# Folding a small matrix into two weight matrices: 128-row matmuls replaced by 32-row tiles of TensorE

## The chip, the cores and the metric

The kernel runs on one core of one Trainium2 chip. The metric is the device time of one execution in microseconds (us). "PE" is TensorE's matmul stream, "PEld" its weight loads, DVE is VectorE, ACT is ScalarE.

## The reference, cut to what matters

Two branches over the same input are mixed by a gate. The part that the change touches is the feature map of the attention branch:

```python
qkv = (x @ wqkv)...                               # x: 2048 x 512, 32 heads of 16
pq = jnp.einsum('bhsd,hdf->bhsf', q, w_phi)       # w_phi: 32 heads, 16 x 16 each
pk = jnp.einsum('bhsd,hdf->bhsf', k, w_phi)
phi_q = concat([softmax(pq), softmax(-pq)])       # the same for pk
```

The kernel never forms `q` and `k`. It multiplies `w_phi` into the weights first: `wq_p = wq @ blockdiag(w_phi)` and `wk_p` likewise, each 512 x 512. The block-diagonal matrix has blocks of 16 x 16, so a 128 x 128 piece of it is zero outside eight blocks. These two products are "the folds".

The other branch computes `z = gelu(x @ w_in)` in two halves, here called z1 and z2, in 16 row tiles each. The folds are woven between these z tiles.

## The kernel before: the parts that matter

The first stage uses eight banks of PSUM (TensorE's output memory): two singly ("pq", two turns) and six in pairs ("zp", three turns in rotation).

```python
def zp_tile():
    return psA.tile([P, 2, CH], FP32, name="zp", tag=next_turn("zp", 3))

def z1_tile(tt):
    zp = z_mm(tt, w_z1, FH)                 # 8 matmuls of 344 columns into a pair
    nc.scalar.activation(out=z1all..., in_=zp[:, :, 0:HF], func=AF.Gelu_apprx_tanh)

def fold(qk, dt):                           # a quarter of one product
    dst = wq_p if qk == 0 else wk_p
    fps = pq_tile([P, CH])
    for kc in range(NDT):                   # 4 matmuls, 128 rows, 128 columns
        nc.tensor.matmul(fps[:, kc * P:(kc + 1) * P],
            lhsT=wqkT[:, qk * 4 + kc, dt * P:(dt + 1) * P],
            rhs=wphi[:, kc, :], start=True, stop=True)
    if dt % 2 == 1:
        nc.scalar.copy(out=dst[:, dt, :], in_=fps[:, :])
    else:
        nc.vector.tensor_copy(out=dst[:, dt, :], in_=fps[:, :])

for c in range(NCH):                        # four chunks of four row tiles
    ts = list(range(c * 4, c * 4 + 4))
    for tt in ts:
        if c > 0: z2_tile(tt)
        if c >= 2 and tt % 2 == 0: fold(3 - c, (tt % 4) // 2)
    for tt in ts:
        z1_tile(tt)
        if c >= 2 and tt % 2 == 0: fold(3 - c, 2 + (tt % 4) // 2)
    z2_norm(ts)
    ...
# The next stage takes PSUM over in new banks. Its first matmuls are k_tile(0), k_tile(1)
# (wk_p, four of 512 columns each) and v_tile(0).
```

The softmax here doesn't subtract the row's maximum and nothing guards it: scores larger than these inputs give would overflow.

## Time and profile before

| | before |
|---|---|
| time, first three runs | 209.02 us median (208.87 to 209.14) |
| span of the profiled run | 207.5 us |
| 32 fold matmuls, PE time they add | 1.79 us (8 x 224 ns) |
| last z matmul to the first v matmul (start to start) | 1.872 us |

From the page of the kernel before, the line of busy times and the line of the chain of waits by engine:

```profile
PE 203.6 (98%) x1456; PEld 122.5 (59%) x1456; DVE 131.4 (63%) x282; ACT 75.4 (36%) x122; POOL 46.6 (22%) x78
PE 98%; DVE 0%; issue 0%
```

PE is busy for 98% of the span and is also 98% of the chain that ended last. A microsecond taken from any other engine is worth nothing unless PE waits for that engine.

The groups of instructions of the folds in the kernel before (line, engine, operation, output<-input, shapes and count, then busy us and mean ns of one, then idle time ahead and its releaser):

```profile
L319 PE MATMUL pq<-wphi,wqkT 128*128 128x128 bf16 x32 | 3.1, 219 | 0.0
L328 DVE CAST wq_p<-pq 128x512 bf16<-128x512 f32 x2 | 1.4, 684 | 1.0 <-PE pq L319 1.0
L328 DVE CAST wk_p<-pq 128x512 bf16<-128x512 f32 x2 | 1.4, 682 | 0.6 <-PE pq L319 0.6
L326 ACT CAST wk_p<-pq 128x512 bf16<-128x512 f32 x2 | 1.2, 580 | 0.0
L326 ACT CAST wq_p<-pq 128x512 bf16<-128x512 f32 x2 | 1.2, 580 | 0.0
```

The 3.1 us of PE are not the cost. The records overlap: each is 219 ns long, and they start 56 ns apart. The chain of waits of the same stretch (start us, us, what) shows what a fold adds:

```profile
25.90 0.88 PE zp L195 x6
26.78 0.22 PE pq L319 x4
27.00 2.34 PE zp L195 x16
29.34 0.22 PE pq L319 x4
29.56 1.46 PE zp L195 x10
```

Four fold matmuls take 0.22 us, so eight groups take 1.79 us. That is the whole sum the change can work on: 0.9% of the time.

The windows view of the stretch with the folds (window, us, then busy us and count of PE, PEld, DVE, ACT and POOL, granted clock, DMA share, GB/s):

```profile
26.50:46.00 19.50, 19.50 (x155) 13.67 (x154) 14.32 (x43) 13.07 (x19) 2.53 (x4) 1.00 1.23 263
```

### The profile page before, as it was taken

How to read it: one execution, taken by the hardware profiler on the slowest of the kernel's cores; microseconds unless marked ns; L12 is line 12 of the kernel's file. 1: busy time of each engine (PE TensorE's matmuls, PEld its weight loads, DVE VectorE, ACT ScalarE, POOL GpSimd, SP SyncE). 2: the span in 40 equal slices, each digit the busy share in tenths (PEclk: the TensorE clock that was granted, in tenths of full speed). 3: DMA queues.
4: the chain of work that ended last, by engine and by line, in shares of the span. 5: the costliest groups of instructions: out<-in, count | busy, mean ns of one | idle time of the engine just before them, and what ended most of it. 6: DMA issues, size and time to landing. Idle time of an engine off the chain costs nothing.

```text
span 207.5 us, 3776 instructions
## 1 busy us (share of the span) xinstructions
PE 203.6 (98%) x1456; PEld 122.5 (59%) x1456; DVE 131.4 (63%) x282; ACT 75.4 (36%) x122; POOL 46.6 (22%) x78
## 2 busy tenths in 40 slices
PE   8999999999999999999999999999999999999994
PEld 4666666765566555556565666555455555665642
DVE  2477786764977777879797788555466563633330
ACT  3665666666422232333323033222251126002322
POOL 7020202020542227243342422222204220200000
PEclk9999999999999999999999999999999999999999
DMA  6999999999922014971403236753564469253442
GB/s 189 263 187 202 242 290 218 267 284 179 290 38 43 0 38 89 254 179 33 92 18 71 50 41 115 144 106 70 108 160 89 76 114 182 56 104 65 132 89 77
DMA packets 88970, 27.20 MB, mean 131 GB/s; under 512 B 82968, under 2 KB 88952, under 8 KB 88952
## 3 DMA queue, kind: packets, MB, share of 16 engines
q1 hardware_dynamic: 86176, 24.37, 59.1%
q10 hardware_dynamic: 2744, 2.60, 4.3%
q8 instruction: 11, 0.18, 0.4%
q14 instruction: 7, 0.06, 0.1%
q0 software_dynamic: 32, 0.00, 0.0%
HBM read 4.41 MB, written 2.10 MB: 31 GB/s over the span
## 4 chain that ended last, share of the span: by engine, by line
PE 98%; DVE 0%; issue 0%
PE mm L457 36%; PE zp L195 18%; PE mm L366 13%; PE mm L496 8%; PE mm L494 7%; PE mm L406 7%; PE at L470 2%; PE kvacc L422 2%; PE zp L226 2%; PE mm L499 1%; PE pq L319 1%; PE pq L284 1%; DVE ob L506 0%; PE pq L305 0%; PE tp L284 0%
## 5 line engine op out<-in xcount | busy, mean ns | idle before, releaser
L457 PE MATMUL mm<-z2all,wspT 128*128 128x344 bf16 x512 | 79.9, 309 | 0.0
L457 PEld LDWEIGHTS <-wspT 128*128 128x128 bf16 x512 | 49.0, 98 | 25.7 <-issue 0.4
L195 PE MATMUL zp<-w_z,xT 128*128 128x344 bf16 (+1 forms) x256 | 40.6, 312 | 0.0
L370 ACT ACTIVATE eq<-mm 128x512 bf16<-128x512 f32 x32 | 17.4, 594 | 51.3 <-POOL eq L383 21.5
L374 DVE TENSOR_REDUCE zs<-eq 128x64 f32<-128x1024 bf16 x16 | 19.5, 1220 | 20.3 <-ACT eq L370 20.3
L195 PEld LDWEIGHTS <-xT 128*128 128x128 bf16 x256 | 24.7, 99 | 11.2
L462 DVE SCALAR_TENSOR_TENSOR ucat<-mm,bT,z1all 128x344 bf16<-128x344 f32 x32 | 17.4, 544 | 21.8 <-PE mm L457 21.8
L383 POOL TENSOR_TENSOR eq<-eq,ratio 128x512 bf16<-128x512 bf16 x16 | 16.9, 1058 | 50.2 <-DVE ratio L382 41.7
L370 ACT ACTIVATE ek<-mm 128x512 bf16<-128x512 f32 x32 | 17.3, 600 | 27.1 <-PE mm L366 27.1
L510 ACT ACTIVATE ob<-mm,g_inv 128x512 bf16<-128x512 f32 (+1 forms) x16 | 10.9, 681 | 32.8 <-PE mm L499 28.3
L374 DVE TENSOR_REDUCE zs<-ek 128x64 f32<-128x1024 bf16 x16 | 19.3, 1209 | 2.8 <-ACT ek L370 2.8
L496 PE MATMUL mm<-wspT,uT 128*128 128x512 bf16 (+2 forms) x85 | 20.1, 366 | 0.0
L366 PEld LDWEIGHTS <-xT 128*128 128x128 bf16 x128 | 12.2, 98 | 12.9 <-PE mm L499 0.8
L383 POOL TENSOR_TENSOR ek<-ek,ratio 128x512 bf16<-128x512 bf16 x16 | 16.9, 1059 | 2.0 <-DVE ratio L382 1.2
L494 PE MATMUL mm<-wspT,oT 128*128 128x512 bf16 (+2 forms) x68 | 16.6, 366 | 0.0
L366 PE MATMUL mm<-wq_p,xT 128*128 128x512 bf16 x64 | 16.4, 379 | 0.0
L406 PE MATMUL mm<-wv_sb,xT 128*128 128x512 bf16 x64 | 16.4, 379 | 0.0
L366 PE MATMUL mm<-wk_p,xT 128*128 128x512 bf16 x64 | 16.3, 379 | 0.0
L213 DVE BATCH_NORM_STATS2 bn<-z2all 128x6 f32<-128x344 bf16 x32 | 14.9, 502 | 0.0
L210 ACT ACTIVATE z2all<-zp 128x688 bf16<-128x688 f32 x16 | 11.8, 744 | 7.3 <-PE zp L195 6.8
L264 ACT ACTIVATE z1all<-zp 128x688 bf16<-128x688 f32 x16 | 11.9, 744 | 6.7 <-PE zp L195 6.7
L496 PEld LDWEIGHTS <-uT 128*128 128x128 bf16 x85 | 8.1, 98 | 9.2
(79 smaller groups left out, 150.9 us busy)
## 6 DMA issues: line engine op xcount, KB each, us to landing
out_dram<-ob ACTq DMA_DIRECT2D x15, 128.0 KB, 1.8
wspT<-in_B_w_out_dram SPq DMA_DIRECT2D x2, 640.0 KB, 5.6
w_z<-in_B_w_in_dram SPq DMA_DIRECT2D x2, 344.0 KB, 4.2
w_z<-in_B_w_in_dram ACTq DMA_DIRECT2D x3, 172.0 KB, 3.5
wv_sb<-in_A_wqkv_dram SPq DMA_DIRECT2D x1, 512.0 KB, 4.7
wspT<-in_A_wo_dram SPq DMA_DIRECT2D x1, 512.0 KB, 6.2
xs<-in_A_x_dram SPq DMA_DIRECT2D x2, 128.0 KB, 3.1
xs<-in_A_x_dram SPq DMA_DIRECT2D x1, 256.0 KB, 4.3
```

What stands on the lines that cost most here:

```text
L195: nc.tensor.matmul(zp[:, j, 0:n], lhsT=xT[:, dt, tt * P:(tt + 1) * P], rhs=wt[:, dt, j * HF:j * HF + n], start=(dt == 0), stop=(dt == NDT ...
L213: nc.vector.bn_stats(out=bn6[:, tt, j, :], in_=z2v[:, j, :])
L264: nc.scalar.activation(out=z1all[:, tt, :].rearrange("p (j n) -> p j n", j=2), in_=zp[:, :, 0:HF], func=AF.Gelu_apprx_tanh,)
L366: nc.tensor.matmul(ps[:, :], lhsT=xT[:, dt, tt * P:(tt + 1) * P], rhs=w[:, dt, :], start=(dt == 0), stop=(dt == NDT - 1))
L370: nc.scalar.activation(out=e[:, :, a, :], in_=ps[:, :].rearrange("p (h f) -> p h f", f=DH), func=AF.Exp, scale=1.0 - 2.0 * a)
L374: nc.vector.tensor_reduce(out=z[:].rearrange("p h a -> p (h a)"), in_=e[:].rearrange("p h a f -> p (h a) f"), axis=AX.X, op=ALU.add,)
L383: nc.gpsimd.tensor_tensor(out=e[:, :, 1, :], in0=e[:, :, 1, :], in1=ratio[:, :, None].to_broadcast([P, H, DH]), op=ALU.mult)
L406: nc.tensor.matmul(v_ps[:, :], lhsT=xT[:, dt, tt * P:(tt + 1) * P], rhs=wv_sb[:, dt, :], start=(dt == 0), stop=(dt == NDT - 1))
L457: nc.tensor.matmul(gp[:, 0:HF], lhsT=wspT[:, st, tt * P:(tt + 1) * P], rhs=z2all[:, st, j * HF:(j + 1) * HF], start=(st == 0), stop=(st == ...
L462: nc.vector.scalar_tensor_tensor(out=ucat[tt % NU][:, c0 + j * HF:c0 + (j + 1) * HF], in0=gp[:, 0:HF], scalar=bT[:, tt:tt + 1], in1=z1all[ ...
L494: nc.tensor.matmul(acc, lhsT=oT[:, g, :], rhs=wo_t[:, g, c0:c1], start=(g == 0), stop=False)
L496: nc.tensor.matmul(acc, lhsT=uT[:, i + ft, :], rhs=w_main[i][:, ft, c0:c1], start=False, stop=False)
```

## The change

A fold's 128 x 128 piece of `w_phi` is cut into its four diagonal 32 x 32 blocks. Each block is a matmul of 32 rows and 32 columns in its own 32-row tile of the array, so that four can run side by side. A fold is now one burst of 64 matmuls, once per weight matrix. Its result, 2048 columns, fills four PSUM banks, hence one z pair and both small banks; each row tile writes a bank of its own. Going from matmuls of the whole array to row tiles, or back, is called a change of mode below. ScalarE copies the pair at once, and the two small banks after two later z1 tiles.

```diff
-    def fold(qk, dt):
...
+    def fold(qk):
+        dst = (wq_p if qk == 0 else wk_p)[:].rearrange("p dt n -> p (dt n)").rearrange(
+            "p (m r f) -> p r m f", r=4, f=32)
+        pair = zp_tile()
+        banks = [pair[:, 0, :], pair[:, 1, :], pq_tile([P, CH])[:, :], pq_tile([P, CH])[:, :]]
+        for m in range(NDT * NDT):
+            dt, kc = divmod(m, NDT)
+            for r in range(4):
+                rows = slice(32 * r, 32 * r + 32)
+                nc.tensor.matmul(
+                    banks[r][:, m * 32:(m + 1) * 32],
+                    lhsT=wqkT[rows, qk * 4 + kc, dt * P:(dt + 1) * P],
+                    rhs=wphi[rows, kc, rows], start=True, stop=True,
+                )
+
+        def take(out, in_):
+            nc.scalar.copy(out=out, in_=in_.rearrange("p (m f) -> p m f", f=32))
+
+        nc.scalar.copy(out=dst[:, 0:2], in_=pair[:, :, :].rearrange("p r (m f) -> p r m f", f=32))
+        return [lambda: take(dst[:, 2], banks[2]), lambda: take(dst[:, 3], banks[3])]
...
-                if c >= 2 and tt % 2 == 0:
-                    fold(3 - c, (tt % 4) // 2)
+                if c >= 2 and tt % 4 == 1:
+                    later = fold(3 - c)
             for tt in ts:
                 z1_tile(tt)
                 if c >= 2 and tt % 2 == 0:
-                    fold(3 - c, 2 + (tt % 4) // 2)
+                    later.pop(0)()
```

More of the change, by code (lines that the diff above doesn't have):

```diff
@@ L313, in wphi_fold @@
         )
-    def fold(qk, dt):
-        dst = wq_p if qk == 0 else wk_p
-        fps = pq_tile([P, CH])
-        for kc in range(NDT):
-            nc.tensor.matmul(
-                fps[:, kc * P:(kc + 1) * P],
-                lhsT=wqkT[:, qk * 4 + kc, dt * P:(dt + 1) * P],
-                rhs=wphi[:, kc, :],
-                start=True, stop=True,
-            )
-        if dt % 2 == 1:
-            nc.scalar.copy(out=dst[:, dt, :], in_=fps[:, :])
-        else:
-            nc.vector.tensor_copy(out=dst[:, dt, :], in_=fps[:, :])
+    def fold(qk):
[16 more added lines that the diff above has]
+        return [lambda: take(dst[:, 2], banks[2]), lambda: take(dst[:, 3], banks[3])]
     with tc.manual_schedule(engines={mybir.EngineType.PE, mybir.EngineType.Activation}):
```

## The prediction

> **What bounds the kernel.** TensorE. The page's busy table gives PE 98% of a 207.5 us span at full clock, and the chain of waits is PE for 98%; in the stretch 26.6–46.0 us, where the folds are, the windows view gives PE 19.40 of 19.40 us (ScalarE 13.1, VectorE 14.3). So only PE's time counts, and evacuation only if PE waits for it.
>
> **Removed.** 32 fold matmuls of 128 rows and 128 columns. In the timeline they start 56 ns apart, their weight loads hidden: 16 x 56 = 0.90 us per fold, 1.79 us in all. Also four VectorE copies of 0.68 us and four ScalarE copies of 0.58 us, none on the chain.
>
> **Added.** 128 matmuls (64 per fold) of 32 rows and 32 columns, each with its own weight load: 13 ns of streaming, four row tiles side by side. Nearest relatives in this trace:
> - The four 64-row remainder groups (line 499): two row tiles start 3–4 ns apart, 512 columns each, so row tiles do overlap. Entering costs 311 − 216 = 95 ns over the normal spacing and leaving about 92: the drain on a mode switch that the Trainium skill ("TensorEngine Tiling (Array Packing)", Key Properties) names. So about 0.19 us per fold.
> - The 68-column matmuls (lines 422, 470): one weight load and one matmul every 30–34 ns, also just after a semaphore instruction had held the sequencer (122.43 us). So an instruction can be issued at least every 16 ns.
>
> The Trainium skill ("TensorE: Matmul & The Clock Gate", Wait — 56ns, not 53.3ns?) puts the floor of one matmul at about 25 ns; no run here shows it. If it holds per row tile: 16 rounds x 25–32 ns = 0.4–0.5 us plus switches = about 0.65 us (estimate), against 0.90. If issue limits instead, the bulk beyond the roughly 17 pairs that PE's queue holds (semaphore instructions run 17 matmuls ahead of execution) costs up to 32 ns a pair: 47 x 32 + 190 = 1.7 us. I expect 0.75 us per fold, a gain of about 0.3 us for both.
>
> **ScalarE and buffers.** The 1024-column piece should take about 1.0 us (extrapolated from 0.58 us for 512 and 0.74 for 688 columns); ScalarE has 3 us idle per fold. The pair uses one turn of the three z buffers; a buffer is free about 1.1 us after its last matmul, and is wanted again 2.3 us or more after it. No stall there.
>
> One new wait: two extra turns shift the z rotation, so the last z1 tile sits in the buffer whose second bank the second k tile takes. Its gelu now ends 46.87 us, that k tile starts 46.79. Allowing for the semaphore, PE waits about 0.15 us, once.
>
> **Sum.** 209.02 − 0.3 + 0.15 = **208.85 us**, 8 in 10 within 208.3–209.9. Faster by over 2%: 0.005; within 2%: 0.985; slower by over 2%: 0.01.
>
> **What would show it.** Fold length on PE (last z matmul before to first after): 0.75 us; 0.65 says tiles overlap fully, over 1 us says issue-bound. Row tiles starting about 4–8 ns apart. Gaps of about 95 ns at each switch. The second k tile's first matmul released by ScalarE's last gelu. ScalarE busier by about 2 us, VectorE less by 2.7, changing nothing.
>
> **What would make it wrong.** Small matmuls issuing slower than 8 ns per instruction (up to +1.6 us); row tiles not overlapping at 32 columns; the strided output slowing the copies; a stall of z tiles behind the 1 us copy.

## More of the kernel before

A z2 tile is also read by VectorE (one gate column), after ScalarE's gelu.

## The result, and the profile after

| | before | after |
|---|---|---|
| time, median of 4 runs | 209.0 us (208.87 to 209.14) | 208.52 us (208.29 to 208.70) |
| ratio | | 0.9976, 95% interval 0.9959 to 0.9994 |
| span of the profiled run | 207.5 us | 206.7 us |

The same lines of the page after, and the groups of the folds:

```profile
PE 202.9 (98%) x1552; PEld 121.2 (59%) x1552; DVE 128.9 (62%) x278; ACT 77.0 (37%) x124; POOL 46.4 (22%) x78
PE 98%; DVE 0%; issue 0%
...
L324 PE MATMUL pq<-wphi,wqkT 32*128 32x32 bf16 x64 | 1.3, 176 | 0.0
L324 PE MATMUL zp<-wphi,wqkT 32*128 32x32 bf16 x64 | 1.3, 176 | 0.0
L331 ACT CAST wk_p<-pq 128x512 bf16<-128x512 f32 x2 | 1.2, 580 | 0.0
L331 ACT CAST wq_p<-pq 128x512 bf16<-128x512 f32 x2 | 1.2, 580 | 0.0
L324 PEld LDWEIGHTS <-wqkT 32*128 32x128 bf16 x128 | 1.1, 91 | 0.6 <-issue 0.6
L333 ACT CAST wk_p<-zp 128x1024 bf16<-128x1024 f32 x1 | 1.0, 1007 | 0.0
L333 ACT CAST wq_p<-zp 128x1024 bf16<-128x1024 f32 x1 | 1.0, 1007 | 0.0
```

The strided output slows the ScalarE copies by nothing: 580 ns for 512 columns, as before. The weight loads have a new idle time, "issue", of 0.6 us in two pieces. That is the entry into each burst, where the weights are not loaded ahead: the first load starts 4 ns before its matmul, against 145 ns in the first fold of before. The windows view of the same stretch after:

```profile
26.50:46.00 19.50, 19.50 (x251) 12.87 (x250) 12.51 (x40) 15.24 (x22) 2.53 (x4) 1.00 1.23 250
```

ScalarE is 2.2 us busier and VectorE 1.8 us less busy in this window. PE stays at 19.50 of 19.50.

The start times in the trace's records resolve the rest to a few ns. All 256 z matmuls are recorded in every trace, so the program can be cut at fixed points. Times are start to start, in us:

| segment | before | after | difference |
|---|---|---|---|
| start of the span to the 17th z matmul | 8.842 | 8.406 | −0.436 |
| 17th to 129th z matmul | 16.602 | 16.602 | 0.000 |
| 129th to last z matmul (the folds) | 20.334 | 19.936 | −0.398 |
| last z to first v matmul (k tiles 0 and 1) | 1.872 | 2.001 | +0.129 |
| first v to last matmul | 156.556 | 156.553 | −0.003 |

The first line must be set aside: no instruction on PE ahead of the 17th z matmul was changed. The change proper is −0.398 + 0.129 = −0.27 us. How PE spends the burst, from the same records ("entry" is the gap before the first fold matmul beyond the usual 146 ns, "exit" the time from the last fold matmul to the next z matmul, the last matmul's own slot included):

| | entry | first to last matmul | exit | total per fold |
|---|---|---|---|---|
| before, one group of 4 (four groups to a fold) | 0 | 168 ns | 56 ns | 224 ns, x4 = 894 ns |
| after, 64 matmuls | 97 ns | 476 ns | 111 ns | 684 ns |

Inside the burst the starts of the four row tiles are 3, 4 and 3 ns apart, and a round of four comes every 25 ns (39 from the first to the second). After 32 matmuls the pace changes: every matmul then comes about 8.3 ns after the one ahead of it, 33.3 ns per round. The second z matmul behind each burst also comes about 10 ns late, so that the 0.42 us that the two folds gain leave 0.40 in the segment. The first burst in the timeline of PE (start us, us, engine, line, operation, output<-input, rows*columns, shape, count; 30 lines like the two of the burst are left out):

```profile
27.06 0.46 PE L195 MATMUL zp<-w_z,xT 128*128 128x344 bf16 x2
27.44 0.19 PE L324 MATMUL zp<-wphi,wqkT 32*128 32x32 bf16 x2
27.45 0.19 PE L324 MATMUL pq<-wphi,wqkT 32*128 32x32 bf16 x2
...
28.03 0.32 PE L195 MATMUL zp<-w_z,xT 128*128 128x344 bf16 x1
```

The new wait of the second k tile shows in the chain of waits. Before, 44 to 48.7 us:

```profile
44.92 1.17 PE zp L195 x8
46.09 1.73 PE mm L366 x8
```

After, the same eight k matmuls take 1.85 us instead of 1.73:

```profile
43.94 1.31 PE zp L195 x9
45.25 1.85 PE mm L372 x8
```

And after, the timeline of ScalarE there (start us, us, engine, line, operation, output<-input):

```profile
45.29 0.74 ACT L264 ACTIVATE z1all<-zp 128x688 bf16<-128x688 f32 x1
46.05 1.28 ACT L376 ACT_TABLE_LOAD   x1
```

The last gelu ends at 46.03 us; the second k tile's first matmul starts at 46.085, and is 348 ns after its predecessor where 216 is usual.

### The profile page after: what moved, and what is told of

It reads as the page before. It is cut to its first block, busy times and chain, and to the rows that moved or that the text cites. A ratio compares the mean times of both kernels' runs of the same rounds, so it can differ in the third digit from the quotient of the medians.

```text
span 206.7 us, 3967 instructions
## 1 busy us (share of the span) xinstructions
PE 202.9 (98%) x1552; PEld 121.2 (59%) x1552; DVE 128.9 (62%) x278; ACT 77.0 (37%) x124; POOL 46.4 (22%) x78
## 4 chain that ended last, share of the span: by engine, by line
PE 98%; DVE 0%; issue 0%
PE mm L463 36%; PE zp L195 18%; PE mm L372 14%; PE mm L502 8%; PE mm L500 7%; PE mm L412 7%; PE at L476 2%; PE kvacc L428 2%; PE zp L226 2%; PE mm L505 1%; PE pq L284 0%; PE zp L324 0%; PE pq L324 0%; DVE ob L512 0%; PE pq L305 0%; PE tp L284 0%
## 5 line engine op out<-in xcount | busy, mean ns | idle before, releaser
L195 PE MATMUL zp<-w_z,xT 128*128 128x344 bf16 (+1 forms) x256 | 39.1, 310 | 0.0
```

The costliest lines, as they stand in the source:

```text
L195: nc.tensor.matmul(zp[:, j, 0:n], lhsT=xT[:, dt, tt * P:(tt + 1) * P], rhs=wt[:, dt, j * HF:j * HF + n], start=(dt == 0), stop=(dt == NDT ...
```

## The experiments

Eleven runs on three chips. Effects of 0.1 to 0.4 us cannot be seen in the times: equal kernels differ by more than 1 us from run to run (before: 208.39 to 210.0 over the rounds). So each verdict rests on the segments of the table above, which repeat to a few ns from trace to trace where nothing was changed. Sums of the three middle segments (17th z to first v matmul), less the 38.808 us of before:

| run | difference to before, us | folds on PE, us (both) | 17th z matmul at, us | time (median), ratio |
|---|---|---|---|---|
| before | 0 | 1.788 | 8.842 | |
| after | −0.27 | 1.369 | 8.406 | 208.52, 0.9976 |
| e0_after_again | −0.27 | 1.367 | 9.628 | 208.84, 0.9989 |
| e1_rot_before | +0.50 | 1.788 | 8.720 | 209.37, 1.0009 |
| e2_after_norot | −0.03 | 1.366 | 8.242 | 208.71, 0.9983 |
| e3_before_act | 0.00 | 1.788 | 9.432 | 209.08, 0.9993 |
| e4_serial | +1.48 | 3.114 | 8.764 | 210.74, 1.0097 |
| e5_64row | −0.30 | 1.340 | 8.028 | 208.32, 0.9973 |
| e6_switch | +1.79 | 3.574 | 8.378 | 210.59, 1.0084 |
| e7_dve | +0.30 | 1.366 | 8.232 | 209.49, 1.0030 |
| e8_unspaced | −0.27 | 1.367 | 9.161 | 208.79, 0.9995 |
| e9_64row_rot | −0.43 | 1.339 | 8.637 | 208.75, 0.9987 |
| e10_128row | +0.13 | 1.788 | 8.334 | 208.76, 0.9984 |

The column "17th z matmul" holds the noise. It lies between 8.03 and 9.63 us, in programs whose PE instructions are the same up to there, and the span follows it: span less this start is 198.61 us for before, 198.34 for after and 198.31 for e0.

### The changed kernel again

No edit.

> The changed kernel once more, to separate its effect from the start-up. In the first pair of traces the two folds together cost PE 1.369 us instead of 1.788 (-0.42), the second k tile waited 0.13 us longer, and the 17th z matmul, which runs before any changed line, started 0.44 us earlier. Theory A (the change is worth -0.42 + 0.13 = -0.29 us, and the start-up difference is chance): mean about 0.29 us under before, 208.7 if before is 209.0; folds again 0.68 us each, the k wait again 0.13 us, and a start of the 17th z matmul anywhere between about 8.4 and 8.9 us. Rival B (the start-up gain belongs to the change): the 17th z matmul again at 8.4 us and 0.5 us or more under before.

Measured: folds 1.367 us, last z to first v 2.001 us, as in the first trace. But the 17th z matmul came at 9.628 us, 0.79 us later than in the trace of before, and outside the 8.4 to 8.9 us expected: the start-up varies more than I thought. The median was 208.84 us against 208.95, ratio 0.9989, interval 0.9961 to 1.0017. Theory A holds and rival B falls: the early start of the first pair of profiles was chance. So the first four runs of each, 0.48 us apart in their medians, overstated the change.

### What the new wait is: two shifts of the rotation

The two folds take two extra turns of the z pairs. In the built programs the last z1 tile therefore sits in banks 2 and 3 instead of 4 and 5, and the second k tile's bank is bank 3 in both. First the kernel before, shifted by two turns and otherwise untouched:

```diff
         for c in range(NCH):
             ts = list(range(c * 4, c * 4 + 4))
+            turn["zp"] += 1 if c < 2 else 0
```

> The kernel before, with its z rotation shifted by two turns (two single skips, early) and nothing else. Theory A: the second k tile now waits for the last gelu, its gap grows from 216 to about 350 ns, and the time by 0.13 us (209.1). Rival (the wait comes of ScalarE's extra copies): gap stays 216 ns, time 209.0.

Measured: last z to first v 2.002 us (before 1.872), the wait of 0.13 us in a kernel whose folds and copies are untouched. So the rotation makes it, not ScalarE's extra work. The time went up by more than 0.13, because the first skip cost 0.374 us between the 17th and the 129th z matmul. The second skip cost nothing.

Then the changed kernel, with one skip, which brings the rotation back:

```diff
         for c in range(NCH):
             ts = list(range(c * 4, c * 4 + 4))
+            turn["zp"] += 1 if c < 1 else 0
```

> The changed kernel with one z buffer turn skipped early, so that the last z1 tile sits where it sat before and the second k tile gets a bank freed earlier. Theory A (the wait is the shifted rotation): the gap before the second k tile's first matmul falls from 348 to 216 ns, folds stay at 0.68 us, nothing else moves: about 0.13 us faster than the changed kernel, some 0.42 us under before. Rival (ScalarE is late because it took over all copies): the gap stays near 348 ns. A reuse of a z buffer after two tiles instead of three, once, should cost nothing: free 1.1 us after its last matmul, wanted after 1.3.

Measured: last z to first v 1.872 us, so the wait is gone, as theory A said. But 16.972 us from the 17th to the 129th z matmul: the skip gave 0.370 us away. The expectation "should cost nothing" was wrong. The timeline of this run names the reason:

```profile
10.78 0.74 ACT L210 ACTIVATE z2all<-zp 128x688 bf16<-128x688 f32 x1 [0.43 <-PE pq L299]
10.79 0.14 DVE L211 COPY glog<-zp 128x1 f32<-128x1 f32 x1
...
10.98 2.79 PE L195 MATMUL zp<-w_z,xT 128*128 128x344 bf16 x18 [0.23 <-DVE glog L211]
```

The skip makes a z1 tile reuse a pair after two tiles whose last user was a z2 tile. A z2 pair is read by ScalarE and then by VectorE for its gate column, and VectorE was behind. I had reckoned with ScalarE alone. After a z1 tile the pair is free with the gelu, which is why the second skip of e1 was free.

### Is it the copies? Two runs that leave the row tiles out

The kernel before with all eight copies on ScalarE:

```diff
-        if dt % 2 == 1:
-            nc.scalar.copy(out=dst[:, dt, :], in_=fps[:, :])
-        else:
-            nc.vector.tensor_copy(out=dst[:, dt, :], in_=fps[:, :])
+        nc.scalar.copy(out=dst[:, dt, :], in_=fps[:, :])
```

> The kernel before, with all eight fold copies on ScalarE, the matmuls as they were. Theory A (evacuation is off PE's path): same time within 0.1 us, folds still 224 ns on PE, eight times; ScalarE busier by 2.3 us, VectorE less by 2.7. Rival C (part of the gain comes from relieving VectorE): 0.2 us or more faster than before.

Measured: the three middle segments are those of before to 1 ns. Relieving VectorE is worth nothing.

Everything of the change except the row tiles:

```diff
-            for r in range(4):
-                rows = slice(32 * r, 32 * r + 32)
-                nc.tensor.matmul(
-                    banks[r][:, m * 32:(m + 1) * 32],
-                    lhsT=wqkT[rows, qk * 4 + kc, dt * P:(dt + 1) * P],
-                    rhs=wphi[rows, kc, rows], start=True, stop=True,
-                )
+            nc.tensor.matmul(
+                banks[dt][:, kc * P:(kc + 1) * P],
+                lhsT=wqkT[:, qk * 4 + kc, dt * P:(dt + 1) * P],
+                rhs=wphi[:, kc, :], start=True, stop=True,
+            )
```

(with plain slices in place of the rearranged copies)

> Everything of the change except the row tiles: one burst of 16 matmuls of 128 rows per fold into one z pair and the two small banks, evacuated by ScalarE in the same three spaced pieces. Theory A (only the row tiles gain): 0.90 us per fold, 1.79 in all as before, and the 0.13 us wait of the second k tile: behind the start-up 0.13 us longer than before. Rival F (grouping and moving the copies gains by itself): as the changed kernel, 0.27 us shorter.

Measured: the folds take 2 x 894 ns, the same 1.788 us as before, and the second k tile waits. The eight k matmuls in its chain of waits:

```profile
45.58 1.86 PE mm L366 x8
```

+0.13 us behind the start-up: the change without its row tiles is a loss. Its time, 208.76 us, is nevertheless under that of before (208.97), with an interval across 1 (0.9963 to 1.0004). Going by the times alone, one would have called it a gain.

### Is it the overlap? The loops exchanged

```diff
-        for m in range(NDT * NDT):
-            dt, kc = divmod(m, NDT)
-            for r in range(4):
+        for r in range(4):
+            for m in range(NDT * NDT):
+                dt, kc = divmod(m, NDT)
```

> The changed kernel with the two loops of a fold exchanged, so that 16 matmuls in a row use the same row tile before the next tile starts: same instructions, same columns, same banks. Theory A (the gain is that four row tiles run side by side): one matmul every 25 ns or more, 64 x 25 + 0.2 = 1.8 us per fold instead of 0.68, about 2.2 us slower than the changed kernel. Rival D (the gain is the quarter of the columns alone): [...]1.2 us per fold, about 1.0 us slower. If overlap plays no part at all: 0.68 us and the same time.

Measured: 1.557 us per fold, against 0.684 in the changed kernel and 0.894 before. The same 64 matmuls, in another order, turn the gain of 0.21 us per fold into a loss of 0.66. The groups of its weight loads and matmuls, to be held against those of after (1.1 and 1.3 us):

```profile
L324 PEld LDWEIGHTS <-wqkT 32*128 32x128 bf16 x128 | 2.9, 91 | 0.6 <-issue 0.6
L324 PE MATMUL pq<-wphi,wqkT 32*128 32x32 bf16 x64 | 1.8, 172 | 0.0
L324 PE MATMUL zp<-wphi,wqkT 32*128 32x32 bf16 x64 | 1.8, 172 | 0.0
```

Within one row tile a matmul starts every 25 ns. The Trainium skill ("TensorE: Matmul & The Clock Gate", section "Wait — 56ns, not 53.3ns?") gives this floor as about 25 ns however few the columns; the trace agrees to the ns. In the first half of the changed kernel's burst a whole round of four row tiles takes the same 25 ns: the floor holds for each row tile by itself. The burst came out shorter than the 1.8 us expected, because around each change of row tile the starts are closer together: records there are 2 to 22 ns apart, and between the second and third row tile those of "pq" lie between those of "zp", so that two row tiles overlap there too. Rival D's 1.2 us is excluded.

### What a burst pays for its mode: one small matmul ahead of each fold

```diff
         fps = pq_tile([P, CH])
+        nc.tensor.matmul(
+            fps[:, 0:32], lhsT=wqkT[0:32, qk * 4, dt * P:(dt + 1) * P],
+            rhs=wphi[0:32, 0, 0:32], start=True, stop=True,
+        )
```

> The kernel before, with one 32-row, 32-column matmul ahead of each of its eight folds, its result overwritten by the fold. Theory A (leaving the 128-row mode and coming back costs about 0.2 us each time): each fold's stretch grows from 224 to about 430 ns, the kernel by 8 x 0.2 = 1.6 us. Rival (no drain; the gaps at the folds come from something else): 15 to 25 ns each, 0.2 us in all.

Measured: each group grew from 224 to 447 ns. In the chain of waits of this run, L318 is the extra matmul and L323 the fold, whose four matmuls took 0.22 us before:

```profile
26.31 0.12 PE pq L318
26.43 0.33 PE pq L323 x4
26.76 2.34 PE zp L195 x16
```

One matmul of 32 columns costs 223 ns, eight of them 1.79 us; the rival's 15 to 25 ns each are excluded. I read this as the drain at a change of tiling mode, which the Trainium skill states without a figure ("TensorEngine Tiling (Array Packing)", Key Properties). The changed kernel pays it twice, in one burst per weight matrix. With the old split into eight groups it would pay 8 x 0.2 us, nearly all that the fold matmuls cost before (an estimate from these numbers; no run has row tiles in eight groups). This is why the folds were gathered, and with that why four banks had to be found.

### How wide should the row tiles be? 64 rows

```diff
-        banks = [pair[:, 0, :], pair[:, 1, :], pq_tile([P, CH])[:, :], pq_tile([P, CH])[:, :]]
+        banks = [[pair[:, 0, :], pair[:, 1, :]], [pq_tile([P, CH])[:, :], pq_tile([P, CH])[:, :]]]
...
-            for r in range(4):
-                rows = slice(32 * r, 32 * r + 32)
+            for r in range(2):
+                rows = slice(64 * r, 64 * r + 64)
                 nc.tensor.matmul(
-                    banks[r][:, m * 32:(m + 1) * 32],
+                    banks[m // 8][r][:, (m % 8) * 64:(m % 8 + 1) * 64],
```

(and the copies with r=2, f=64)

> The changed kernel with 64-row tiles: two row tiles side by side, 64 columns each, 32 matmuls per fold instead of 64, same four banks. In the changed kernel the first rounds of four take 25 ns and the later ones 33.5. Theory A (issue limits the later ones, at 4.2 ns an instruction): with half the instructions every round is array-bound, 16 x 29 ns = 0.47 us, plus 0.2 of switches: 0.67 us per fold, the same time as the changed kernel, and an even pace. Rival (the later pace is a limit of the array or of PSUM writing): the pace changes in mid-burst here too, over 0.75 us.

Measured: 670 ns per fold, half the instructions, and an even pace of one round of two every 29 ns to the end. The result fits theory A: with 32 instead of 64 matmuls the later, slower pace is gone, although each matmul has twice the columns. A limit on the columns streamed or written in one burst is excluded, since this burst has as many. A limit that sets in after 32 matmuls of any kind is not: this burst ends just there. That it is the issue of instructions (4.2 ns each) which limits the second half of the 32-row burst is an inference from these two paces. What makes the pace change just after 64 instructions was not tested.

### Must the copies be spaced?

```diff
-                    later = fold(3 - c)
+                    for piece in fold(3 - c):
+                        piece()
             for tt in ts:
                 z1_tile(tt)
-                if c >= 2 and tt % 2 == 0:
-                    later.pop(0)()
```

> The changed kernel with all three copies at once behind the fold, 2.2 us of ScalarE in a row, instead of spaced over the following tiles. Theory A (the slack of the z buffers covers it: the delayed gelu ends 3.2 us after the fold, its buffer is wanted at 3.5): PE waits nowhere new, same time as the changed kernel. Rival E (the spacing is needed): z tiles wait for buffers, 0.3 to 1 us slower, with new PE gaps between z tiles after each fold.

Measured: the three middle segments are those of the changed kernel within 3 ns. ScalarE's timeline behind the first fold of this run:

```profile
28.94 1.01 ACT L333 CAST wk_p<-zp 128x1024 bf16<-128x1024 f32 x1
29.84 1.09 ACT L331 CAST wk_p<-pq 128x512 bf16<-128x512 f32 x2
30.79 1.42 ACT L210 ACTIVATE z2all<-zp 128x688 bf16<-128x688 f32 x2
32.50 0.74 ACT L264 ACTIVATE z1all<-zp 128x688 bf16<-128x688 f32 x1 [0.29 <-PE zp L195]
```

The copies hold ScalarE for 2 us and two gelus run late, but by 32.2 us it has caught up, and PE never waited for them. The spacing, a part of the change's name, is worth nothing here.

### Must it be ScalarE?

```diff
-            nc.scalar.copy(out=out, in_=in_.rearrange("p (m f) -> p m f", f=32))
+            nc.vector.tensor_copy(out=out, in_=in_.rearrange("p (m f) -> p m f", f=32))
...
-        nc.scalar.copy(out=dst[:, 0:2], in_=pair[:, :, :]...)
+        nc.vector.tensor_copy(out=dst[:, 0:2], in_=pair[:, :, :]...)
```

> The changed kernel with the three pieces copied by VectorE instead of ScalarE. Theory A (evacuation counts only where PE waits for its buffer): the pair takes about 1.2 us on a VectorE that also runs the statistics of the z2 tiles, so it may be freed only about 2.4 us after the fold, and it is wanted 2.3 us after: a wait of 0 to 0.5 us per fold at the first z1 tile, nothing else; folds 0.68 us. Rival (the engine is of no account): no wait, same time. Rival G (ScalarE is essential): over 0.5 us per fold.

Measured: the folds are unchanged, but two z1 tiles behind each fold start late, by 0.12 and 0.17 us: 0.57 us in all, more than the row tiles had gained. VectorE's timeline behind the first fold, which ended at 27.9 us:

```profile
28.15 0.16 DVE L211 COPY glog<-zp 128x1 f32<-128x1 f32 x1
28.23 0.93 DVE L213 BATCH_NORM_STATS2 bn<-z2all 128x6 f32<-128x344 bf16 x2
29.07 1.21 DVE L333 CAST wk_p<-zp 128x1024 bf16<-128x1024 f32 x1
30.19 0.20 DVE L214 BATCH_NORM_AGGREGATE mv<-bn 128x2 f32<-128x12 f32 x1
30.31 1.23 DVE L331 CAST wk_p<-pq 128x512 bf16<-128x512 f32 x2
31.46 0.15 DVE L211 COPY glog<-zp 128x1 f32<-128x1 f32 x1
```

The pair's copy starts 1.2 us after the fold, behind the statistics of the z2 tile, and the gate copy of a later z2 pair waits until 31.46 us behind the pieces. Both pairs come free late. So with this order of work the copies can't all go to VectorE; the pair on ScalarE with the two small pieces on VectorE was not tried. The 0.29 us per fold lie inside theory A's 0 to 0.5 us and under rival G's, but theory A foresaw only the first of the two waits.

### Both repairs together

64-row tiles, and one skip where the pair's last user is a z1 tile:

```diff
         for c in range(NCH):
             ts = list(range(c * 4, c * 4 + 4))
+            turn["zp"] += 1 if c == 1 else 0
```

> The combination that the traces point to: 64-row tiles (fold 0.670 us against 0.684) and one z buffer turn skipped, but at the start of the second chunk, where a z1 tile, not a z2 tile, was the buffer's last user: the run that shifted the kernel before skipped there too and lost nothing by it, while the skip one chunk earlier cost 0.37 us. Theory A: 2 x 0.670 for the folds, 1872 ns from the last z matmul to the first v matmul as in the kernel before, 16.60 us from the 17th to the 129th z matmul: PE's program behind the start-up 0.43 us shorter than before and 0.16 us shorter than the changed kernel; about 208.4 if before is 208.85. Rival: the skip costs 0.37 us here too.

Measured: 670 ns per fold, 16.602 us from the 17th to the 129th z matmul, 1.872 us from the last z to the first v matmul: −0.43 us against before and −0.16 us against the changed kernel, as expected. It beats both in the program behind the start-up. The times can't show it: 208.75 us against 208.97, ratio 0.9987, interval 0.9968 to 1.0005.

### The start-up

Ahead of the 17th z matmul two things vary in the traces. One is when the first matmuls come up to full speed: the last z matmul with a long record (over 350 ns, where 309 is usual) starts at 6.50 us in the trace of before, at 4.64 in that of after, and there is none in e5. The Trainium skill ("TensorE: Matmul & The Clock Gate", Part 1) says that the clock is released by a free-running window of activity, so that the point varies by ±500 ns from run to run; these traces agree that it varies, but by more (6.50 against 4.64 us), and they do not show the window. The other is a weight load from memory. The chain of waits of e3, which started late, opens with it:

```profile
1.74 5.45 DMA w_z<-in_B_w_in_dram
7.19 0.04 issue
7.23 1.33 PE zp L195 x8
```

In the trace of before nothing waits there. Neither goes with the change: in the kernels with 128-row folds (before, e1, e3, e10) the 17th z matmul came between 8.33 and 9.43 us, in those with row tiles between 8.03 and 9.63.

## Why the prediction was right, point by point

- **The bound.** Right. PE is 98% of the chain in both kernels, and e3 and e8 show that other engines' time is worth nothing while PE does not wait for it.
- **The fold.** Predicted 0.75 us, where 0.65 would say that "tiles overlap fully"; measured 0.684. The gain for both is 0.42 us, not 0.3. The step that was mis-sized is the burst: I allowed for an issue limit beyond about 17 queued pairs and up to 32 ns a pair. The slower pace set in only after 32 pairs and was 8.3 ns a pair. It cost 8 rounds x 8.3 ns = 67 ns per fold.
- **Mode switches.** Predicted 95 and 92 ns from the 64-row groups of the same trace; measured 97 and 111, the second with the last matmul's own slot of about 8 ns in it. e6 measures the two, with one small matmul, at 223 ns.
- **Row tiles side by side.** Predicted 4 to 8 ns between starts; measured 3 to 4 ns, then 8.3. e4 shows that the gain rests on it.
- **ScalarE and buffers.** Predicted 1.0 us for the pair and no stall; measured 1.007 us and none. ScalarE is 2.2 us busier in the stretch (predicted 2), VectorE 1.8 us less busy there and 2.5 us on the whole page (predicted 2.7). Right.
- **The new wait.** Predicted 0.15 us at the second k tile from the banks and the gelu's end; measured 0.13. e1 makes it in the kernel before by the rotation alone.
- **The sum.** Predicted −0.17 us (the terms as written add up to −0.15); the program became 0.27 us shorter. The measured median, 208.52 us, lies 0.33 us under the predicted one, and inside its range. The range alone proves little: no change at all would have been inside it too. What bears the prediction out is the segments. About 0.1 us of the 0.33 is the burst; the rest is within the spread of the start-up, which the prediction did not name. The three runs of before within 0.27 us of each other had made the spread look small. Over the later rounds before alone went from 208.39 to 210.0 us.

## What to carry to other kernels

In this kernel row tiles paid because matmuls of different row tiles alternate and many of them are gathered behind one change of mode: 64 small matmuls in a burst saved 0.21 us and one alone cost 0.22 us. When a burst borrows a buffer out of a rotation, follow the rotation to its end: who sits where in the next stage cost a third of the gain here (0.13 of 0.42 us). For effects smaller than the spread of the times, cut the traces at fixed instructions and compare the segments.

## What the Trainium skill lacked or had wrong

- "TensorEngine Tiling (Array Packing)", Key Properties, names the drain at a change of tiling mode but no size: 97 ns to enter and 111 to leave for a 32-row burst, 97 and 122 for a 64-row one (from the start of the last small matmul), 223 ns for a single 32-row matmul in between 128-row ones.
- "TensorE: Matmul & The Clock Gate", Back-to-back issue gap, has the floor of 25 ns, which e4 confirms, but not that it holds per row tile: four row tiles of 32 columns share one round of 25 ns, two of 64 columns one of 29 ns.
- The same page, Part 3, models a pack of tiles by about 4 ns per tile. The trace agrees (3 to 4 ns) for the first 32 matmuls of a burst. No page has the pace that follows, 8.3 ns for a weight load and a matmul. The page's queue of 64 entries would fit the place of the change, but semaphore instructions in the trace of before run at most 17 matmuls ahead of execution, so this stays open.
- The same page, Part 3, says that a weight load overlaps matmuls in flight only when the row group differs. In e4 weight loads (91 ns) and matmuls (171 ns) of one and the same row tile alternate every 25 ns, so their records do overlap (the ends of matmul records are modelled); the same page's "background weight buffer" (in the mechanism of Part 3 and in Step-by-step) fits this better.
